# A two-weight spectral filter with a gate: a new order list with other read positions, a second unit with summed products, and four folds on GpSimd

## The chip, the cores and the metric

The kernel runs on one core of a Trainium2 chip. The metric is the device time of one execution in microseconds (us), the median of several runs. The core has a matrix engine (TensorE, PE in the profile), a vector engine (VectorE, DVE), an engine for activations and copies (ScalarE, ACT), a general one (GpSimd, POOL), and SyncE (SP), which here issues nearly all DMAs. Each engine takes its own instructions in program order and waits on semaphores for the others. Matrix products go to PSUM (eight banks of 128x512 f32); ScalarE and VectorE bring them back to SBUF, which is called evacuation here.

## The reference

Two spectral filters act on the same input, and a gate mixes them:

```python
def filt(x, w_r, w_i):                       # x: 1 x 2048 x 1024
    X = rfft2(x.astype(float32))
    X = X * (w_r + 1j * w_i)                 # weights: 2048 x 513
    return irfft2(X, s=(2048, 1024)).astype(bfloat16)

def reference(A_x, A_w_r, A_w_i, B_x, B_w_r, B_w_i, gate_w):
    x = A_x
    g = sigmoid((x * gate_w).sum(-1, keepdims=True))
    return g * filt(x, A_w_r, A_w_i) + (1 - g) * filt(x, B_w_r, B_w_i)
```

B_x is not used. All data are bf16.

## The kernel before

The transform of x is made once and multiplied by four weight planes (real and imaginary part of A and B). Column frequencies are split in an even half (par 0) and an odd half (par 1); row frequencies in 8 units for each half, so there are 16 units n, 0 to 7 even, 8 to 15 odd. The work has three stages.

- Head. x comes in 16 tiles. `V` (line 277, `xfold`) adds and subtracts the two column halves of a tile on VectorE; `f` is the first row transform of such a folded tile for both halves; `r` is the same from the raw tile, with matmuls of twice the width and no fold; `E` and `O` do one half each for a pair of tiles. The results are evacuated to y. `y` prepares the gate's weights.
- Units. `F` (f2, line 365) is the column transform of a unit, `G` (f3) the twiddle and second row transform, with the constant WF; `d` (edge) the products of an edge column; `c` (cmul, line 415) multiplies the unit by its four weight planes in one VectorE operation; `i n.r` (i1) is the first inverse row transform, real part r = 0 and imaginary r = 1, with the constant WI. `a` (part, line 439) adds two of the product planes on VectorE first, so that both i1 of that unit need three matmul terms instead of four. After `i n.1` the unit is written to a scratch in DRAM. For an even unit, GpSimd writes one column of the weights (L369) before `F`; it waits for the unit's weights. `h` and `g` make the gate and put it in the matrix EAB.
- Output. `q half.g.v` (fetch, line 470) reads the scratch back in another layout: q0 into xr (the memory of x), q1 into ro. `j half.v` (i2) is the second inverse row transform with the gate in it, `k` (i3) the inverse column transform, `s` (fold, line 551) adds and subtracts its cosine and sine parts, `D` (i3d) does k and s at once in matmuls for the odd half, `t` (last, lines 565 and 574) adds and subtracts the halves and writes to the output.

The order on every engine follows one list written out by hand, ORDER. Behind the colon stand the engines of a step's evacuations: A ScalarE, V VectorE; AV is first half and second half. In `k`, H leaves the sine part in PSUM for the fold to read there. For `s`, V is VectorE and Q is GpSimd, which cannot read PSUM. BANKS gives the PSUM bank of every product and SLOTS the buffer of every T, X, p, V and rl tile in order: there are two T, two X, four p, four V and four rl. A step that takes a buffer waits for its last readers.

SyncE issues in program order: x, then the constants and the weights W0 to W6 and W10 to W13 (lines 234 to 251), and then what the list says: the scratch writes, the late weights `w`, the reads `q`, the constant IGU (`l`), the outputs. A DMA whose condition isn't met holds back all behind it. Weights n = 7, 8, 9, 14, 15 reuse memory of x and of earlier weights. In the program, the reads q1.g.v need the scratch writes of four odd units: q1.0.v of units 8 to 11, q1.1.v of units 12 to 15; j1.0 and j1.1 need q1.0.0 and q1.1.0, j1.2 and j1.3 need q1.0.1 and q1.1.1, and so on.

Of the kernel before, what the change touches and what calls it, by code (L numbers as in the profile page):

```python
# [11 lines left out]
S = 2048  # L12
# [14 lines left out]


ORDER = """
V0 V1 V3 f0:AA f1:VA r2:AA V4 f3:VA V7 r5:AV V9 f4:AA r6:VA f7:VA r8:VA f9:VA r11:AA V13 r10:VA r12:AV f13:AA E14:VA y  # L30
O14:VA F0:AA F1:AA d0 G0:AA F2:AA d1 c0 G1:AA F3:AA d2 c1 G2:AA h F4:AA d3 G3:AA i0.0:AA i0.1:AA w7 c2 d4 c3 F5:AV
G4:AA i1.0:AA i2.0:VA c4 i2.1:AV d5 G5:AA i1.1:VA F6:AA F7:AA d6 w9 G6:AA i3.0:AA c5 i3.1:AV d7 F8:AA w8 c6 g0 i5.0:AA
G7:AV G8:AA w15 i5.1:AV q0.0.1 w14 c7 i6.0:AA q0.0.3 F9:AA F10:AA i4.0:AA c8 i6.1:VA i7.0:AA G9:AV G10:AV i4.1:VA
i7.1:AA c10 F11:AA q0.0.0 F12:AV c9 g1 G11:AA q0.0.2 c11 F13:AA G12:AA q0.1.0 i10.0:AA i9.0:AA i8.0:VA q0.1.3 i10.1:VV
i9.1:AA c12 i8.1:AA i11.0:VA G13:AA q0.1.1 q0.1.2 F14:VA F15:AA j0.0:AA c13 G14:AA i12.0:AV G15:AA i12.1:AA i11.1:AA
c14 c15 i13.0:AA i13.1:AA i14.0:AV a15.1:V i14.1:VV k0.0:HA j0.3:AA i15.0:AV i15.1:AV j0.2:AV j0.5:AA s0.0:V l q1.0.0
k0.3:HA j0.1:AA q1.1.0 s0.3:V j0.4:VA k0.5:HA j0.7:AA q1.0.1 s0.5:V k0.1:HA q1.1.1 k0.4:HA j0.6:AA s0.1:V k0.2:HA
s0.4:V q1.0.2 q1.1.2 k0.7:AA k0.6:HA j1.0:AA q1.1.3 s0.2:V j1.1:VA s0.6:V q1.0.3 k1.0:AA s0.7:V k1.1:HA s1.0:V j1.2:AA
j1.3:AA t0.2 s1.1:V D2:AA j1.4:AA k1.3:AA t2.2 t1.2 j1.5:AA s1.3:V D4:AA t3.2 t4.2 j1.6:AA D5:AA t5.2 D6:AA j1.7:AA
t6.0:S t6.1:S D7:AAAP t7.0:A t7.1:S  # L40
"""


# [1 line left out]


BANKS = """
01234567013245760321564371052634710562437162057143057623057146257146251427306517306514273065142763051427630154
62073154620731546207315426701354270615342706135427061354027364107236410752643071265401326470152647031564703125
64703125647  # L50
"""

SLOTS = {"T": "010101010101010101001010", "X": "0101010101001010", "p": "012302132103102130213021301",
         "V": "30123012302301230123", "rl": "0123012301231023102310321032103"}


def _bf16np(a):
# [99 lines left out]
def gated_mix(ctx, tc, x_in, we_in, wo_in, first_in, out):  # L157
    nc = tc.nc
    cn = make_constants()
    dr = {n: nc.inline_tensor(a, name=f"cst_{n.lower()}").ap() for n, a in cn.items() if n not in ("F1", "SG")}  # L160
# [13 lines left out]
    slots = {t: [wk.tile([P, w], BF16, name=f"{t}_{k}") for k in range(n)] for t, (n, w) in width.items()}  # L174
    order = {t: iter(v) for t, v in SLOTS.items()}

# [19 lines left out]
    F1 = const.tile([P, 208], BF16, name="f1")  # L196
# [10 lines left out]
    WF = const.tile([P, NT, 3, 64], BF16, name="wf")  # L207
    WI = const.tile([P, NT, 4, 64], BF16, name="wi")
# [5 lines left out]
    y = [Y[:, par] for par in range(2)]  # L214
# [3 lines left out]
    def load_w(n):  # L218
        par, u = n // NU, n % NU
        if n == 7:  # L220
            w = XP[0][:, 0:2064]
        elif 10 <= n < 14:
            w = wod[n - 10][:]
        else:
            k = {8: 0, 9: 1, 14: 2, 15: 3}.get(n, n)
            w = RP[k // 2][:, 2064 * (k % 2):2064 * (k % 2) + 2064]
        w = w[:, 0:8 * PIT[par]].rearrange("p (t a m) -> p t a m", t=2, a=4)
        nc.sync.dma_start(w, w_in[par][u])
        Ws[n] = w
# [4 lines left out]
    nc.sync.dma_start(fdv(0), dr["FD"][:, 0])  # L234
    nc.sync.dma_start(WF[:, 0:4], dr["WF"][:, 0:4])
    load_w(0)
    nc.sync.dma_start(WI[:, 0:4], dr["WI"][:, 0:4])
    load_w(1)
    load_w(2)
    nc.sync.dma_start(WF[:, 4:16], dr["WF"][:, 4:16])  # L240
    load_w(3)
    nc.sync.dma_start(WI[:, 4:16], dr["WI"][:, 4:16])
    load_w(4)
# [420 lines left out]
```

## Time and profile before

| | us |
|---|---|
| median of 3 runs (lowest, highest) | 107.3 (106.96, 108.08) |
| profiled execution | 107.58 |
| its span, first to last instruction | 105.8 |

| engine | busy us (share of the span) | instructions |
|---|---|---|
| TensorE | 96.9 (92%) | 1606 |
| VectorE | 90.7 (86%) | 141 |
| ScalarE | 93.6 (89%) | 187 |
| GpSimd | 10.1 (10%) | 14 |

The mean granted clock of TensorE is 0.996. The DMA queue of SyncE carried 36.37 MB in 16128 packets, 92.3% of the time of 16 DMA engines.

In the rows of the order of time, a row begins with its start and its length in us, merges neighbours of one kind (x16 is sixteen instructions), and ends with the idle time in front of it and what ended that idle time. An arrow reads output from input: `ro<-sc` is a read of the scratch into ro. Instructions of one engine overlap a little, so a ScalarE evacuation of 128x512 is 0.6 to 0.8 us long and the next starts 0.5 us after it. On ScalarE such rows are L263, on VectorE L265.

### The profile page before, as it was taken

What the parts mean: (1) busy time and instruction counts of PE and PEld (TensorE: products, weight loads), DVE (VectorE), ACT (ScalarE), POOL (GpSimd) and SP (SyncE); (2) the same over time, 40 slices, a digit from 0 to 9 for tenths busy, and PEclk for the clock granted to TensorE, in tenths of its full rate; (3) what the DMA queues carried; (4) which work ended last, traced back from release to release, by engine and by line L of the source; (5) the groups of instructions that cost most, each with busy time, mean ns of one, the idle gap of its engine ahead of it and who ended that gap; (6) DMA issues with size and microseconds to landing.
All of it is one profiled execution on the core that took longest, in us unless ns stands there. A gap on an engine that the chain in (4) does not pass through costs nothing. (4 is left out here: it accounts for less than half of the span.)

```text
span 105.8 us, 3917 instructions
## 1 busy us (share of the span) xinstructions
PE 96.9 (92%) x1606; PEld 66.5 (63%) x1608; DVE 90.7 (86%) x141; ACT 93.6 (89%) x187; POOL 10.1 (10%) x14
## 2 busy tenths in 40 slices
PE   5999999969999999999999999999999698999740
PEld 2299998635655766655765567667898485754520
DVE  1399877388999989999999999999989969899870
ACT  5069999997999999999999999999999888999730
POOL 1000001179880000000000000000000000000000
PEclk9999999999999999999999999999999999999998
DMA  2999999999999999999999799969999899967993
GB/s 50 395 421 421 386 358 353 413 428 396 398 405 409 401 375 359 395 356 345 386 373 403 223 376 379 373 249 340 321 278 298 338 353 418 397 259 321 389 352 120
DMA packets 16737, 37.06 MB, mean 350 GB/s; under 512 B 1612, under 2 KB 10448, under 8 KB 15696
## 3 DMA queue, kind: packets, MB, share of 16 engines
q1 hardware_dynamic: 16128, 36.37, 92.3%
q10 hardware_dynamic: 560, 0.45, 1.3%
q8 instruction: 12, 0.20, 0.7%
q14 instruction: 5, 0.04, 0.1%
q0 software_dynamic: 32, 0.00, 0.0%
HBM read 24.23 MB, written 12.58 MB: 348 GB/s over the span
## 5 line engine op out<-in xcount | busy, mean ns | idle before, releaser
L453 PE MATMUL pt<-p,wi 64*64 64x512 bf16 x504 | 30.1, 377 | 0.2 <-DVE rl L265 0.2
L263 ACT CAST rl<-pt 128x512 bf16<-128x512 f32 x47 | 25.9, 732 | 0.1
L415 DVE TENSOR_TENSOR p<-X,ro 128x4096 bf16<-128x4096 bf16 x11 | 25.2, 2297 | 0.4 <-ACT X L263 0.3
L263 ACT CAST T<-pt 128x512 bf16<-128x512 f32 (+1 forms) x40 | 21.8, 636 | 0.9 <-PE pt L532 0.5
L453 PEld LDWEIGHTS <-wi 64*64 64x64 bf16 x504 | 15.3, 106 | 10.4 <-issue 0.9
L263 ACT CAST V<-pt 128x512 bf16<-128x512 f32 x29 | 17.3, 748 | 1.1 <-PE pt L483 1.1
L263 ACT CAST X<-pt 128x512 bf16<-128x512 f32 x29 | 16.8, 682 | 0.1
L375 PE MATMUL pt<-fd,y 128*128 128x256 bf16 x128 | 15.9, 273 | 0.0
L263 ACT CAST y<-pt 128x512 bf16<-128x512 f32 x21 | 10.9, 649 | 3.9 <-PE pt L297 3.4
L375 PEld LDWEIGHTS <-y 128*128 128x128 bf16 x128 | 11.6, 98 | 4.2 <-issue 2.9
L265 DVE CAST rl<-pt 128x512 bf16<-128x512 f32 x17 | 11.3, 683 | 0.0
L498 PE MATMUL pt<-ig,V 128*128 128x256 bf16 x88 | 10.8, 273 | 0.0
L369 POOL TENSOR_SCALAR ro<-ro 128x8 bf16<-128x8 bf16 x7 | 8.7, 1244 | 21.4 <-DMA ro<-in_we_dram 21.4
L574 DVE TENSOR_TENSOR rl<-wo,T 128x1024 bf16<-128x1024 bf16 (+1 forms) x16 | 8.9, 620 | 0.6 <-ACT T L263 0.6
L394 PE MATMUL pt<-T,wf 64*64 64x512 bf16 (+2 forms) x192 | 9.4, 307 | 0.0
L263 ACT CAST p<-pt 128x512 bf16<-128x512 f32 x14 | 9.4, 823 | 0.0
L551 DVE TENSOR_TENSOR wo<-p,pt 128x512 bf16<-128x512 bf16 x14 | 8.8, 682 | 0.6 <-ACT p L263 0.5
L415 DVE TENSOR_TENSOR p<-X,wo 128x4096 bf16<-128x4096 bf16 x4 | 9.1, 2285 | 0.0
L498 PEld LDWEIGHTS <-V 128*128 128x128 bf16 x88 | 8.0, 98 | 1.5 <-issue 0.4
L265 DVE CAST y<-pt 128x512 bf16<-128x512 f32 x11 | 7.2, 686 | 0.4 <-PE pt L309 0.4
L306 PE MATMUL pt<-f,xr 64*128 64x256 bf16 x112 | 7.0, 269 | 0.0
L394 PEld LDWEIGHTS <-wf 64*64 64x64 bf16 x192 | 4.7, 107 | 3.0 <-issue 0.4
(58 smaller groups left out, 97.2 us busy)
## 6 DMA issues: line engine op xcount, KB each, us to landing
sc<-rl SPq DMA_DIRECT2D x16, 512.0 KB, 5.2
xr<-sc SPq DMA_DIRECT2D x8, 512.0 KB, 6.5
ro<-sc SPq DMA_DIRECT2D x8, 512.0 KB, 6.5
ro<-in_we_dram SPq DMA_DIRECT2D x7, 516.0 KB, 9.0
xr<-in_x_dram SPq DMA_DIRECT2D x7, 512.0 KB, 6.1
out_dram<-rl SPq DMA_DIRECT2D x6, 512.0 KB, 3.1
wo<-in_wo_dram SPq DMA_DIRECT2D x4, 512.0 KB, 7.5
ro<-in_wo_dram SPq DMA_DIRECT2D x4, 512.0 KB, 6.5
```

Of the source, the lines that this page charges most:

```text
L263: nc.scalar.copy(out=out, in_=in_)
L265: nc.vector.tensor_copy(out=out, in_=in_)
L306: nc.tensor.matmul(pv[h][:, :, c, :, :].rearrange("p a e k -> p e a k"), lhsT=xs(j0, h, q), rhs=fs(h, 0, *st), start=(q == 0), stop=(q == 3))
L369: nc.gpsimd.tensor_scalar(Ws[n][:, :, :, 257:258], Ws[n][:, :, :, 256:257], -1.0, None, ALU.mult)
L375: nc.tensor.matmul(ps[tt][:, e * 256:e * 256 + 256], lhsT=y[par][:, c, e, t].rearrange("p b s k -> p (b s k)"), rhs=FD[:, par, c, e, :], s ...
L394: nc.tensor.matmul(ps[tt][ho, dst:dst + ln], lhsT=WF[hp(j), 2 * u + tt, w, :], rhs=T[hp(j), tt, src:src + ln], start=(k == 0), stop=(k == 2))
L415: nc.vector.tensor_tensor(po, xo, wo, ALU.mult)
L453: nc.tensor.matmul(ps[tt][hp(j), :], lhsT=WI[hin, 2 * u + tt, w, :], rhs=p[hin, q, tt, a::2, o:o + 256], start=(k == 0), stop=(k == len(te ...
L498: nc.tensor.matmul(po, lhsT=V[:, s, 2 * r + c, :], rhs=IG[:, par, 2 * r + c, :], start=(c == 0), stop=(c == 1))
L551: (nc.vector if eng == "V" else nc.gpsimd).tensor_tensor(ev[:, :, r, :], c_, s_, op)
L574: nc.vector.tensor_tensor(o4[:, k, h] if not isinstance(od, list) else o4[:, k.start, h], x, y_, op)
```

## The change

The list ORDER is replaced as a whole, with its BANKS and SLOTS, and two constants change places in the SyncE queue. By count, the lists differ in this:

- `V` 7 to 6, `f` 7 to 6, `r` 7 to 8; the pair done by E and O is tiles 10 and 11 and not 14 and 15.
- `a` 1 to 2: units 1 and 5 in place of unit 15.
- `k` with H 8 to 2. `s` on VectorE 11 to 7; s0.0, s0.3, s0.5 and s0.7 are on GpSimd.
- `t1` goes out in halves.
- Evacuations on ScalarE 180 to 179, on VectorE 37 to 44, seven of these in `k`.
- All j and k stand behind i15.1 (before, j0.0, j0.3 and k0.0 stood ahead of it); the q1 reads stand in the list right behind it.
- WF[4:16] is issued ahead of W1, and WI[0:4] behind W2.

```diff
 ORDER = """
-V0 V1 V3 f0:AA f1:VA r2:AA V4 f3:VA V7 r5:AV V9 f4:AA r6:VA f7:VA r8:VA f9:VA r11:AA V13 r10:VA r12:AV f13:AA E14:VA y
-O14:VA F0:AA F1:AA d0 G0:AA F2:AA d1 c0 G1:AA F3:AA d2 c1 G2:AA h F4:AA d3 G3:AA i0.0:AA i0.1:AA w7 c2 d4 c3 F5:AV
-G4:AA i1.0:AA i2.0:VA c4 i2.1:AV d5 G5:AA i1.1:VA F6:AA F7:AA d6 w9 G6:AA i3.0:AA c5 i3.1:AV d7 F8:AA w8 c6 g0 i5.0:AA
-G7:AV G8:AA w15 i5.1:AV q0.0.1 w14 c7 i6.0:AA q0.0.3 F9:AA F10:AA i4.0:AA c8 i6.1:VA i7.0:AA G9:AV G10:AV i4.1:VA
-i7.1:AA c10 F11:AA q0.0.0 F12:AV c9 g1 G11:AA q0.0.2 c11 F13:AA G12:AA q0.1.0 i10.0:AA i9.0:AA i8.0:VA q0.1.3 i10.1:VV
-i9.1:AA c12 i8.1:AA i11.0:VA G13:AA q0.1.1 q0.1.2 F14:VA F15:AA j0.0:AA c13 G14:AA i12.0:AV G15:AA i12.1:AA i11.1:AA
-c14 c15 i13.0:AA i13.1:AA i14.0:AV a15.1:V i14.1:VV k0.0:HA j0.3:AA i15.0:AV i15.1:AV j0.2:AV j0.5:AA s0.0:V l q1.0.0
-k0.3:HA j0.1:AA q1.1.0 s0.3:V j0.4:VA k0.5:HA j0.7:AA q1.0.1 s0.5:V k0.1:HA q1.1.1 k0.4:HA j0.6:AA s0.1:V k0.2:HA
-s0.4:V q1.0.2 q1.1.2 k0.7:AA k0.6:HA j1.0:AA q1.1.3 s0.2:V j1.1:VA s0.6:V q1.0.3 k1.0:AA s0.7:V k1.1:HA s1.0:V j1.2:AA
-j1.3:AA t0.2 s1.1:V D2:AA j1.4:AA k1.3:AA t2.2 t1.2 j1.5:AA s1.3:V D4:AA t3.2 t4.2 j1.6:AA D5:AA t5.2 D6:AA j1.7:AA
-t6.0:S t6.1:S D7:AAAP t7.0:A t7.1:S
+V0 r1:AA f0:VV V5 V6 r3:AA r4:AV V8 f5:VA r2:VA f6:VA r7:AA f8:AA E10:VA r9:AA V13 V14 r12:VA f13:AA r15:VA f14:AV y
+O10:AA F0:VA F1:AA d0 G0:VA c0 F2:AA d1 G1:AA F3:AA d2 G2:AA F4:AA c1 i0.0:AA w8 d3 a1.0:V i0.1:AA d4 G4:AA c2 i1.0:AA
+c4 G3:AA w7 i1.1:AA F5:AA h F6:AA c3 d5 G5:VA c5 i2.0:AA i2.1:AA i3.0:VA i3.1:AV d6 a5.0:V G6:AA F7:AA w15 F8:AA c6
+i4.0:AV d7 w9 G7:AA i4.1:AA F9:VA q0.0.3 G8:AA i5.0:AA c7 i6.0:VA F10:AA q0.0.1 c8 G9:AA i7.0:AV G10:AA q0.0.2 i5.1:AV
+i7.1:AA c9 i6.1:VV c10 w14 F11:AA F12:AA g0 i8.0:AA i8.1:AA G12:VA i9.0:VA i9.1:VA q0.1.2 q0.1.1 G11:AA F13:AA F14:AA
+c12 q0.1.0 c11 i10.0:VA G13:AA q0.0.0 i12.0:AA c13 G14:AA F15:AA i11.0:AA q0.1.3 i11.1:AV i10.1:AV c14 G15:AA c15
+i13.0:AV i12.1:AA i13.1:AA g1 i14.0:AV i14.1:AA i15.0:AV i15.1:VA q1.0.0 j0.1:AV q1.0.1 q1.1.0 q1.1.1 q1.1.2 l j0.2:VA
+j0.0:VA j0.7:AV k0.1:VV j0.5:AA k0.2:HA j0.6:AA k0.0:VA s0.1:V s0.0:Q j0.3:VA k0.5:AA k0.6:HA s0.2:V j0.4:AA k0.3:AA
+q1.0.2 k0.7:AA s0.6:V s0.5:Q k0.4:VV j1.0:AA s0.4:V j1.1:AA q1.0.3 k1.0:VV q1.1.3 s1.0:V j1.2:AA k1.1:AA t0.2 j1.3:AA
+s1.1:V D2:AA t1.0:S j1.4:AA t1.1:S t2.2 k1.3:AA s1.3:V j1.5:AA D4:AA s0.3:Q j1.6:AA t3.2 D5:AA t4.2 t5.2 s0.7:Q D6:AA
+j1.7:AA t6.0:S t6.1:S D7:AAAP t7.0:A t7.1:S
 """
...
     nc.sync.dma_start(WF[:, 0:4], dr["WF"][:, 0:4])
     load_w(0)
-    nc.sync.dma_start(WI[:, 0:4], dr["WI"][:, 0:4])
+    nc.sync.dma_start(WF[:, 4:16], dr["WF"][:, 4:16])
     load_w(1)
     load_w(2)
-    nc.sync.dma_start(WF[:, 4:16], dr["WF"][:, 4:16])
+    nc.sync.dma_start(WI[:, 0:4], dr["WI"][:, 0:4])
     load_w(3)
     nc.sync.dma_start(WI[:, 4:16], dr["WI"][:, 4:16])
     load_w(4)
```

More of the change, by code (lines that the diff above doesn't have):

```diff
@@ L47 @@
 BANKS = """
-01234567013245760321564371052634710562437162057143057623057146257146251427306517306514273065142763051427630154
-62073154620731546207315426701354270615342706135427061354027364107236410752643071265401326470152647031564703125
-64703125647
-"""
-SLOTS = {"T": "010101010101010101001010", "X": "0101010101001010", "p": "012302132103102130213021301",
-         "V": "30123012302301230123", "rl": "0123012301231023102310321032103"}
+01234567012345617350264173502614735026147362735014736214507362145073162703162037614527615240376152403761524037
+56124750613247506134257061342706153427063125470612547036215473062517340516724051726403175264037152643071526430
+71526430715
+"""
+SLOTS = {"T": "010100101010110101010101", "X": "0101010101010101", "p": "012301230132010321032102323",
+         "V": "30123012301301230123", "rl": "012301230123012310232103210321"}
 def _bf16np(a):
```

## The prediction

> **What bounds it now.** I began with the page's busy shares: TensorE 92%, ScalarE 89%, VectorE 86%, the DMA engines at tenths of 9 nearly throughout. With three engines this full the question is where each of them still waits, so I read the order of time of each engine next. ScalarE first:
>
> ```profile
> 6.10 8.23 ACT L263 CAST y<-pt 128x512 bf16<-128x512 f32 x16 [3.44 <-PE pt L297]
> ...
> 25.27 0.58 ACT L344 CAST V<-pt 128x512 bf16<-128x512 f32 x1 [0.78 <-PE pt L341]
> ...
> 84.99 1.56 ACT L263 CAST V<-pt 128x512 bf16<-128x512 f32 x3 [0.66 <-PE pt L483]
> ...
> 88.48 2.05 ACT L263 CAST V<-pt 128x512 bf16<-128x512 f32 x4 [0.43 <-PE pt L483]
> ...
> 100.38 1.26 ACT L263 CAST T<-pt 128x256 bf16<-128x256 f32 x3 [0.26 <-ACT V L263]
> ```
>
> Columns: start, length, engine, line, operation, count, and in brackets the idle time before it. From 6.10 to 101.64 ScalarE idles about 3.0 us in all, of which these rows show 0.78, 0.66, 0.43 and 0.26. It is the chain that paces the kernel, and a wait that goes or comes on it is worth its length. TensorE gives the reasons:
>
> ```profile
> 14.80 1.95 PE L309 MATMUL pt<-f,xr 64*128 64x128 bf16 x64
> 16.73 1.91 PE L375 MATMUL pt<-fd,y 128*128 128x256 bf16 x16
> ...
> 22.71 0.20 PE L425 MATMUL pt<-T,wf 64*64 64x2 bf16 x4 [0.93 <-DMA wf<-cst_wf]
> ...
> 23.30 1.91 PE L341 MATMUL pt<-y,gwz 128*32 128x512 bf16 x32
> ...
> 74.53 1.11 PE L483 MATMUL pt<-eab,xr 128*128 128x64 bf16 x32
> ...
> 84.56 1.09 PE L483 MATMUL pt<-eab,ro 128*128 128x64 bf16 x32 [0.94 <-DMA ro<-sc]
> ...
> 88.05 1.09 PE L483 MATMUL pt<-eab,ro 128*128 128x64 bf16 x32 [0.45 <-DMA ro<-sc]
> ```
>
> The constant WF lands at 22.7, TensorE stands 0.93 us, the gate products (L341) come late, and that is ScalarE's 0.78. The reads of the odd half (ro<-sc) make TensorE stand 0.94 and 0.45, and that is ScalarE's 0.66 and 0.43. The profiled execution took 107.58 us, span 105.8; the median of the runs, 107.3, is 0.28 lower. I sum against 107.58 and take 0.28 off at the end.
>
> **Work that goes and comes.** Counted over both lists.
> - ScalarE: 180 plain evacuations become 179. Sixteen of them took 8.23 us, so they lie 0.5 us apart: -0.5, on the pacing chain.
> - TensorE: one raw `r` more and one folded `f` less. An `f` took 0.44 us (7.23 to 7.67), an `r` 0.88: +0.44. One more summed unit leaves out 8 of 32 matmuls, about 0.055 us each (112 in a row took 6.21): -0.44. Together 0.
> - VectorE: seven folds stay of eleven, two of them with a PSUM operand where eight had one. Six PSUM folds in a row took 3.68, 0.60 apart; two SBUF folds 0.75, 0.34 apart. Eleven cost 16 x 0.60 + 6 x 0.34 = 11.6, seven cost 4 x 0.60 + 10 x 0.34 = 5.8: -5.8. Seven more evacuations at 0.60: +4.2. One folding of x less, -0.7, one product sum more, +0.6, t1 in halves, +0.1. Together -1.6. VectorE is not the pacing engine, so this is cover and not gain.
>
> **Head of the list.** Now `r1` needs no folding and starts ScalarE 0.75 us earlier. But the last two x tiles were issued by 5.0 and took 9.6 us, so land at 14.6, and TensorE's 14.80 row already hugs that. In the new list V14 (x 14) stands on VectorE ahead of its evacuations of r12, r15 and f14, 0.6 each, so F0 comes at about 16.9 where it came at 16.73: 0, with +0.4 as the other end.
>
> **WF ahead of WI.** WF[4:16] passes W1, W2 and WI[0:4] on the SP queue, so lands about 4 us earlier (three transfers of 516, 516 and 256 KB at some 400 GB/s). WI[0:4] then lands about when WF did, 22.7, and i0.0 wants it at 23. W1 comes up to 1 us later, for d1, behind c0. So the 0.93 and with it ScalarE's 0.78 go: -0.8, other end 0. But what is late next? d4 now stands on VectorE before c2 (it stood after), and needs W4, which no reordering moves:
>
> ```profile
> 17.32 0.27 POOL L369 TENSOR_SCALAR ro<-ro 128x8 bf16<-128x8 bf16 x1 [16.29 <-DMA ro<-in_we_dram]
> ...
> 21.31 1.87 POOL L369 TENSOR_SCALAR ro<-ro 128x8 bf16<-128x8 bf16 x1 [1.00 <-DMA ro<-in_we_dram]
> 24.02 2.23 POOL L369 TENSOR_SCALAR ro<-ro 128x8 bf16<-128x8 bf16 x1 [0.83 <-DMA ro<-in_we_dram]
> ...
> 27.25 2.12 POOL L369 TENSOR_SCALAR ro<-ro 128x8 bf16<-128x8 bf16 x2 [0.32 <-DMA ro<-in_we_dram]
> ```
>
> One operation for each unit of the even half, released by its weights (W0, W2, W3, W4 and W5 here): W4 at 27.25. Then c2 starts at about 27.7 (26.73 before) and ends at 30.0; G3's evacuation needs the X slot c2 frees, and ScalarE gets there at about 29.2: +0.8. Ends: 0 if ScalarE is later, +1.3 if all of VectorE's wait passes on.
>
> **Reads that follow each other.** Two of the odd reads (q1.0.0, q1.0.1) now go out behind the last scratch write; only q1.1.0 waits for that write (issued 75.53, q1.1.0 at 80.32, data at 84.56). So j1.0's data still come some 10.0 us after TensorE's last i1 matmul. But j0.0, j0.3 and k0.0, which ran before that point, now lie behind it: eight j at 0.44 and eight k at 0.87 fill 10.5 us. j1.2's reads now stand one 512 KB transfer (1.3 us) nearer, at 12.2 instead of 13.5, where TensorE has 12.2 us of work. Both waits are covered: -1.1 on ScalarE, other end 0.
>
> **Four groups on GpSimd.** Eight sums of 128x512. The trace has no such row. Its memsets took 0.10 us for 1 element and 0.31 for 256, 0.82 ns an element: 0.52 us if three streams run side by side, 1.36 if in turn; I take 0.95, the middle, as nothing is nearer to either. GpSimd itself has room (10% busy, nothing after 40 us). The price lies on VectorE. Against the third and fourth rows above stand these:
>
> ```profile
> 20.75 2.30 DVE L415 TENSOR_TENSOR p<-X,ro 128x4096 bf16<-128x4096 bf16 x1
> ...
> 23.82 2.30 DVE L415 TENSOR_TENSOR p<-X,ro 128x4096 bf16<-128x4096 bf16 x1
> ```
>
> GpSimd's 0.27 us became 1.87 and 2.23, ending at 23.18 and 26.25, each 0.13 after the VectorE product ended: a VectorE operation with two SBUF inputs keeps GpSimd out until it is done. I take the same for the other direction, which no row shows. (The Trainium skill, "SBUF — State Buffer", section "Who interferes with whom", calls the pair of ports that the two share an exclusive lock that whichever starts first keeps for its whole instruction; the rows agree for VectorE first. Its "GPSIMD Engine Reference", section "Elementwise — side-by-side cycle accounting", has 2.6 cycles an element at 1.2 GHz, an estimate of 1.1 us for 512 elements; by that the sum below would be +0.1, not -0.35.) GpSimd is busy about 7.6 us from k0.0's evacuation on. In that time come VectorE's folds with both inputs in SBUF: s0.1, s0.4 and s1.0. At one blocked GpSimd operation for each: 3 x 0.95 = 2.85, less the 1.6 of cover: +1.25. Behind them on VectorE stand k1.0's evacuation and t0.2, and TensorE's banks behind those. Ends: 3 x 0.52 is inside the cover, 0; 4 x 1.36 - 1.6 = +3.8.
>
> **Sum.** -0.5 - 0.8 + 0.8 - 1.1 + 1.25 = -0.35: 107.2 in such an execution, 106.9 against the median.
>
> **Rivals.**
> - GpSimd's sums stay inside VectorE's cover. For it: VectorE idles 2.6 us in that stage as it is. -0.5 - 0.8 + 0.8 - 1.1 = -1.6: 105.7, down to 104.9 without the wait at G3. Chance 0.30.
> - Slower: GpSimd becomes VectorE's gate. Four waits of 1.36 make +3.8 in place of +1.25, so +2.2: 109.5. It decides from 3.2 us of blocked time on (1.6 of cover and 1.6 of gain), and is over 1% from 4.3. For it: a second fold of a pair finds the next GpSimd sum already queued; against: the folds from PSUM have one SBUF input. Chance 0.20.
> - The head loses: F0 0.4 later, W4's whole 1.3, ScalarE's 0.78 back by another wait. -0.5 + 0.4 + 1.3 - 1.1 + 1.25 = +1.35: 108.6. For it: VectorE now takes V6, V8 and V14 before evacuations that are ready. Chance 0.12.
> - The reads do pause: q1.1.0's wait is still there, and if j and k run faster than counted, -1.1 falls away: +0.75, 108.0. Chance 0.05.
>
> **How the numbers follow.** Forecast 106.9, chance 0.33, its own range 106.2 to 107.9. About 1% (1.1 us) is what a measurement here tells from no change. Faster by more: the first rival, 0.30. Within: forecast and last rival, 0.38. Slower: the other two, 0.32. The range 105.2 to 109.4 takes in the forecast, the head, the reads, most of the first rival and the near part of the second.
>
> **What would show it.** Right: no idle on ro<-sc before L483 near 84; no idle on WF near 22; ScalarE idle before an X evacuation near 29; GpSimd's L551 rows near 0.95 us, and L551 rows of VectorE from SBUF stretched beside them. Wrong: GpSimd's rows over 1.3 us with VectorE idle or stretched by more than 3.2 us after 78; F0 later than 17.2; or ScalarE's idle sum after 30 us above the 1.8 it has now, from banks or slots I did not follow.

## The result and the profile after

| | before | after |
|---|---|---|
| median, us (22 runs each, on the same chips) | 107.58 | 108.02 |
| ratio, 95% interval | | 1.0057 [1.0036, 1.0077] |
| profiled execution, us | 107.58 | 107.82 |
| its span, us | 105.8 | 105.7 |
| device time less span, us | 1.78 | 2.12 |

The change made the kernel slower by 0.6%, some 0.6 us. Four of the 22 runs of the kernel before (109.4 to 110.7 us) fell in a slower state and are left out of the ratio; the median of the others is 107.49. Half of the 0.6 us does not lie between the first and the last instruction at all: device time less span has a median of 2.11 us over the runs of the changed kernel (2.05 to 2.15), and of 1.77 to 1.79 over those of the kernel before. The span itself grew by 0.2 to 0.35 us in the medians (105.9 against 105.55 to 105.7 in the several series) and is about equal in the two profiled executions. So an equal span hides gains and losses that have to be found stage by stage.

The page of the changed kernel, first its engines with busy time and instruction counts, then the one new group of instructions:

```profile
PE 97.9 (93%) x1598; PEld 67.7 (64%) x1600; DVE 91.0 (86%) x141; ACT 93.2 (88%) x186; POOL 18.6 (18%) x22
...
L551 POOL TENSOR_TENSOR wo<-p 128x512 bf16<-128x512 bf16 x8 | 9.4, 1212 | 37.5 <-ACT p L263 37.5
```

GpSimd took eight sums off VectorE, and yet VectorE is as busy as before (91.0 against 90.7). Next the order of time of ScalarE after the change, the main rows with idle time from the head on:

```profile
11.42 7.21 ACT L263 CAST y<-pt 128x512 bf16<-128x512 f32 x14 [0.19 <-PE pt L306]
...
30.05 1.07 ACT L263 CAST X<-pt 128x512 bf16<-128x512 f32 x2 [0.38 <-DVE p L415]
...
76.21 1.07 ACT L263 CAST V<-pt 128x512 bf16<-128x512 f32 x2 [0.17 <-PE pt L483]
...
84.46 3.08 ACT L263 CAST V<-pt 128x512 bf16<-128x512 f32 x6 [0.32 <-PE pt L483]
...
90.79 1.07 ACT L263 CAST T<-pt 128x512 bf16<-128x512 f32 x2 [1.29 <-DVE rl L574]
```

The wait of 0.78 near 25 is gone, and those of 0.66 and 0.43 near 85 have shrunk to one of 0.32 (the 0.17 at 76.21 stands behind a product of the even half, which waits for no odd read). In their place stand 0.38 at 30.05 (the X evacuation of G3, which waits for c2) and 1.29 at 90.79. The second is the largest: the evacuation of D2 into a T buffer waits for VectorE's t0.2 (L574), which still reads it. With 0.62 us in three short waits of the head and 0.26 ahead of the last T the idle time adds up to 3.0 us, as before. TensorE in order of time:

```profile
14.89 0.44 PE L297 MATMUL pt<-f,rl 64*128 64x128 bf16 x9 [0.19 <-issue]
15.13 1.07 PE L306 MATMUL pt<-f,xr 64*128 64x256 bf16 x16
16.00 0.64 PE L297 MATMUL pt<-f,rl 64*128 64x128 bf16 x16
16.45 1.09 PE L309 MATMUL pt<-f,xr 64*128 64x128 bf16 x32
17.64 1.91 PE L375 MATMUL pt<-fd,y 128*128 128x256 bf16 x16
...
22.61 0.20 PE L425 MATMUL pt<-T,wf 64*64 64x2 bf16 x4
...
84.03 1.09 PE L483 MATMUL pt<-eab,ro 128*128 128x64 bf16 x32 [0.17 <-issue]
```

F0 (L375) begins at 17.64 where it began at 16.73: behind the last x tiles TensorE now has f13, r15, f14 and O10 in a row, from 14.9 on. At 22.61 nothing waits for WF. At 84.03 the first product of the odd reads waits 0.17 us where it waited 0.94. The row names nothing that ended this wait ("issue" means that the profile shows no releaser), but the time of the read does: q1.1.0, issued at 79.22, lands 4.7 us later, at 83.94, and the weight load of that product (PEld) starts 0.06 us after it:

```profile
84.00 1.00 PEld L483 LDWEIGHTS <-ro 128*128 128x128 bf16 x32 [0.42 <-issue]
```

In the kernel before, the same read lands at 84.42 and the load starts at 84.53. So the read still decides when the odd half begins; only the wait for it is shorter. And VectorE, in the stretch that leads up to ScalarE's 1.29:

```profile
83.46 1.29 DVE L265 CAST p<-pt 128x512 bf16<-128x512 f32 x2 [0.89 <-PE pt L498]
84.79 1.84 DVE L551 TENSOR_TENSOR wo<-p 128x512 bf16<-128x512 bf16 x2
...
87.86 1.51 DVE L551 TENSOR_TENSOR T<-p 128x512 bf16<-128x512 bf16 x2
89.41 1.29 DVE L574 TENSOR_TENSOR rl<-wo,T 128x1024 bf16<-128x1024 bf16 x2
```

A pair of folds from SBUF took 0.75 before. Here s0.4 takes 1.84 and s1.0 takes 1.51. GpSimd at that time, beside its earlier writes of weight columns:

```profile
27.02 0.43 POOL L369 TENSOR_SCALAR ro<-ro 128x8 bf16<-128x8 bf16 x1 [0.98 <-DMA ro<-in_we_dram]
...
79.32 9.43 POOL L551 TENSOR_TENSOR wo<-p 128x512 bf16<-128x512 bf16 x8 [37.53 <-ACT p L263]
```

Its eight sums run from 79.32 to 88.75 without a gap; the first stretched pair lies inside that time and the second begins in it. One by one, three of these four folds took 0.55, 1.37 and 1.17 us, and each ended 0.28 us after the end of a GpSimd sum; the fourth, behind the last sum, took 0.41, the usual time. Two of the sums beside them took 1.33 us in place of 1.15. The first row is W4, which lands near 27 as it did before.

### The profile page after: what moved, and what is told of

It is laid out like the page before. It is cut to its first block, busy times and chain, and to the rows that moved or that the text cites. A ratio compares the mean times of both kernels' runs of the same rounds, so it can differ in the third digit from the quotient of the medians.

```text
span 105.7 us, 3918 instructions
## 1 busy us (share of the span) xinstructions
PE 97.9 (93%) x1598; PEld 67.7 (64%) x1600; DVE 91.0 (86%) x141; ACT 93.2 (88%) x186; POOL 18.6 (18%) x22
## 4 chain that ended last, share of the span: by engine, by line
PE 87%; DVE 6%; ACT 2%; issue 1%; DVEq 0%; ACTq 0%
PE pt L453 27%; PE pt L375 14%; PE pt L498 9%; PE pt L394 7%; PE pt L483 7%; PE pt L532 7%; PE pt L306 5%; PE pt L195 3%; PE pt L297 2%; DVE y L265 2%; PE pt L341 2%; DVE rl L565 2%; PE pt L357 1%; ACT V L263 1%; DVE rl L574 1%
## 5 line engine op out<-in xcount | busy, mean ns | idle before, releaser
L263 ACT CAST rl<-pt 128x512 bf16<-128x512 f32 x47 | 28.4, 855 | 0.0
L263 ACT CAST T<-pt 128x512 bf16<-128x512 f32 (+1 forms) x41 | 23.0, 690 | 1.8 <-DVE rl L574 1.3
L263 ACT CAST X<-pt 128x512 bf16<-128x512 f32 x29 | 18.6, 774 | 0.4 <-DVE p L415 0.4
L375 PE MATMUL pt<-fd,y 128*128 128x256 bf16 x128 | 16.0, 273 | 0.1
L551 POOL TENSOR_TENSOR wo<-p 128x512 bf16<-128x512 bf16 x8 | 9.4, 1212 | 37.5 <-ACT p L263 37.5
L263 ACT CAST V<-pt 128x512 bf16<-128x512 f32 x27 | 15.0, 669 | 0.5 <-PE pt L483 0.5
L375 PEld LDWEIGHTS <-y 128*128 128x128 bf16 x128 | 11.5, 98 | 4.7 <-issue 3.3
L369 POOL TENSOR_SCALAR ro<-ro 128x8 bf16<-128x8 bf16 x7 | 7.0, 1000 | 22.4 <-DMA ro<-in_we_dram 22.3
L394 PE MATMUL pt<-T,wf 64*64 64x512 bf16 (+2 forms) x192 | 10.5, 307 | 0.1
L574 DVE TENSOR_TENSOR rl<-wo,T 128x1024 bf16<-128x1024 bf16 (+1 forms) x18 | 9.1, 568 | 0.6 <-ACT T L263 0.5
L306 PE MATMUL pt<-f,xr 64*128 64x256 bf16 x128 | 8.4, 279 | 0.0
L394 PEld LDWEIGHTS <-wf 64*64 64x64 bf16 x192 | 5.5, 106 | 3.9 <-issue 0.8
L306 PEld LDWEIGHTS <-xr 64*128 64x128 bf16 x128 | 6.2, 98 | 1.7 <-DMA xr<-in_x_dram 0.8
```

The source lines that it names most:

```text
L263: nc.scalar.copy(out=out, in_=in_)
L306: nc.tensor.matmul(pv[h][:, :, c, :, :].rearrange("p a e k -> p e a k"), lhsT=xs(j0, h, q), rhs=fs(h, 0, *st), start=(q == 0), stop=(q == 3))
L375: nc.tensor.matmul(ps[tt][:, e * 256:e * 256 + 256], lhsT=y[par][:, c, e, t].rearrange("p b s k -> p (b s k)"), rhs=FD[:, par, c, e, :], s ...
L394: nc.tensor.matmul(ps[tt][ho, dst:dst + ln], lhsT=WF[hp(j), 2 * u + tt, w, :], rhs=T[hp(j), tt, src:src + ln], start=(k == 0), stop=(k == 2))
L551: (nc.vector if eng == "V" else nc.gpsimd).tensor_tensor(ev[:, :, r, :], c_, s_, op)
L574: nc.vector.tensor_tensor(o4[:, k, h] if not isinstance(od, list) else o4[:, k.start, h], x, y_, op)
```

## The experiments

My theory after this reading: GpSimd's sums hold up VectorE's folds from SBUF, that passes on through the T buffer to ScalarE, and it eats what WF and the reads bring; the head's lateness is a second loss. Rivals: the wait is one for a buffer and goes with a third T; VectorE needs the relief, so that without GpSimd it would be worse; the head is the loss. Ratios are to the kernel before, with 95% intervals, spans are medians.

**The four groups back on VectorE.**

```diff
-s0.0:Q s0.5:Q s0.3:Q s0.7:Q
+s0.0:V s0.5:V s0.3:V s0.7:V
```

> The four folds go back from GpSimd to VectorE, in the changed list as it stands. If VectorE's folds s0.4 and s1.0 were stretched (1.84 and 1.51 us instead of 0.75) because GpSimd's sums held them, they take 0.75 again; but VectorE gets 4 x 0.67 = 2.7 us more, of which s0.3 and s0.7 stand late in the list: the last t is about 1 us later, ratio to the kernel before 1.010 to 1.020. If GpSimd had been no hindrance, the full 2.7 us show, 1.03. If the 0.3 us that the changed kernel has more outside its span (2.1 us against 1.8) come from GpSimd's eight sums, they are gone here.

Measured: 0.9935 [0.9905, 0.9965], 106.66 us, span 104.85, and 1.79 us outside the span. It is faster than both kernels, so my expectation was wrong, and so was the rival by which VectorE needs the relief. VectorE of this kernel:

```profile
85.11 0.76 DVE L551 TENSOR_TENSOR wo<-p 128x512 bf16<-128x512 bf16 x2
...
87.10 0.76 DVE L551 TENSOR_TENSOR T<-p 128x512 bf16<-128x512 bf16 x2
87.89 1.29 DVE L574 TENSOR_TENSOR rl<-wo,T 128x1024 bf16<-128x1024 bf16 x2
```

and its ScalarE:

```profile
89.28 1.07 ACT L263 CAST T<-pt 128x512 bf16<-128x512 f32 x2
```

Both pairs are back at 0.76, t0.2 begins 1.52 us earlier (87.89 against 89.41), and D2's evacuation follows at 89.28 with no wait, 1.51 earlier. VectorE does eight sums more here, about 2.7 us at the 0.34 apart of the prediction, and is busy 91.7 instead of 91.0: the 1.85 us by which GpSimd stretched its folds paid for most of that.

**The two stretched folds read PSUM.** With one input in PSUM a fold needs one evacuation less and takes 0.6 instead of 0.34.

```diff
-k0.4:VV k1.0:VV
+k0.4:HV k1.0:HV
```

> k0.4 and k1.0 leave their sine part in PSUM for the fold, so that s0.4 and s1.0 have one SBUF input. If GpSimd's sums hold only VectorE operations with two SBUF inputs, these folds take 2 x 0.60 us unstretched, t0.2 comes 1.5 to 2 us earlier, ScalarE's wait of 1.29 us for D2's buffer falls below 0.4, and the span shrinks by 0.5 to 1.2 us (ratio to before 0.995 to 1.001). If the wait for D2's buffer is a matter of the buffers or of VectorE's amount of work alone, nothing changes (1.006), for VectorE's work is the same within 0.1 us.

Measured: 0.9986 [0.9959, 1.0014], 107.21 us, span 104.9, 2.10 outside. VectorE and then GpSimd of this kernel:

```profile
84.87 1.28 DVE L551 TENSOR_TENSOR wo<-p,pt 128x512 bf16<-128x512 bf16 x2
...
87.75 1.29 DVE L551 TENSOR_TENSOR T<-p,pt 128x512 bf16<-128x512 bf16 x2
```

```profile
79.69 9.07 POOL L551 TENSOR_TENSOR wo<-p 128x512 bf16<-128x512 bf16 x8 [37.94 <-ACT p L263]
```

GpSimd's eight sums still run beside both pairs (to 88.76, 0.3 us before the second pair ends), and the pairs take 1.28 and 1.29, what PSUM pairs took before the change (1.28). D2's wait is gone, and the span is that of the kernel without GpSimd, 104.9 against 104.85. So it is not GpSimd as such that costs span here, but GpSimd beside folds that take both inputs from SBUF.

**A third T buffer, which D2 takes.**

```diff
-"T": (2, 1024)
+"T": (3, 1024)
-"T": "010100101010110101010101"
+"T": "010100101010110101210101"
```

> D2 gets a third T buffer, so that its evacuation need not wait until t0.2 has read the old one. The stretch of s0.4 and s1.0 stays at about 1.9 us. If the buffer is the whole way by which the stretch reaches the end, ScalarE's 1.29 us wait goes and the span shrinks by about 1 us; if VectorE itself is full by then (it idles only 0.47 and 0.19 us after 84.8), the wait goes and the span shrinks by 0.2 to 0.6 us at most.

Measured: 1.0006 [0.9979, 1.0032], 107.37 us, span 105.5, 1.91 outside. The folds are stretched as before (1.85 and 1.51), D2 does not wait, but ScalarE does a little later:

```profile
96.17 2.30 ACT L263 CAST T<-pt 128x512 bf16<-128x512 f32 x4 [0.87 <-DVE rl L574]
```

The buffer is how the delay gets from VectorE to ScalarE, not where it comes from: with it taken away two thirds of the wait (0.87 of 1.29) come back at the next T.

**Two of the four groups on GpSimd** (s0.0 and s0.5 stay, which come first).

```diff
-s0.3:Q s0.7:Q
+s0.3:V s0.7:V
```

> The changed kernel with s0.0 and s0.5 on GpSimd and s0.3 and s0.7 on VectorE again. GpSimd is then done at about 83.9 us, before VectorE's folds with two SBUF inputs come (84.8 and later). If only the meeting costs, s0.4 and s1.0 take 0.75 us again and the span is that of the kernel without GpSimd (104.5) or up to 0.7 us less; time outside the span shows what the presence of GpSimd's sums costs: 0.1 to 0.35 us. If GpSimd's sums cost something wherever they stand, the ratio stays near 1.000.

Measured: 0.9996 [0.996, 1.0031], 107.27 us, span 105.2, 2.08 outside. GpSimd is done at 84.55 us, the pairs behind it take 0.76 each, and D2 does not wait: no meeting, no stretch, as expected. The span, expected at 104.5 or below, lies 0.35 us above that of the kernel without GpSimd and 0.7 below that of the changed kernel; the 0.35 is no larger than span differences that stay unexplained further down, so it is not put down to the two groups.

**One group on GpSimd in the kernel before.**

```diff
-s0.7:V
+s0.7:Q
```

> The kernel before with one group, s0.7, on GpSimd, two sums of 128x512. If full-sized late sums lengthen the time outside the span, 1.9 to 2.1 us; s1.0, the next VectorE fold, has one SBUF input here and should not be stretched, so the span stays within 0.3 us of before.

Measured: 0.9965 [0.9931, 0.9999], 107.25 us, span 105.4 (median), 1.79 outside. GpSimd:

```profile
83.83 2.26 POOL L551 TENSOR_TENSOR wo<-p 128x512 bf16<-128x512 bf16 x2 [43.88 <-ACT p L263]
```

One group costs nothing and may bring 0.3%. VectorE of this kernel folds from PSUM until 84.5 and then waits 1.10 us for TensorE. So where no fold from SBUF runs beside them, these sums on GpSimd show no price.

**The head of the kernel before.** Its first lines replace the new ones, first with the banks of before, then with banks renamed so that the steps behind it find the same ones free as in the changed kernel.

```diff
-V0 r1:AA f0:VV V5 V6 r3:AA r4:AV V8 f5:VA r2:VA f6:VA r7:AA f8:AA E10:VA r9:AA V13 V14 r12:VA f13:AA r15:VA f14:AV y
-O10:AA
+V0 V1 V3 f0:AA f1:VA r2:AA V4 f3:VA V7 r5:AV V9 f4:AA r6:VA f7:VA r8:VA f9:VA r11:AA V13 r10:VA r12:AV f13:AA E14:VA y
+O14:VA
```

> The head of the list (x foldings, f, r, E, O, with their banks and buffers) is that of the kernel before, the rest as changed. If the head costs what its rows show (F0 at 17.64 us instead of 16.73), F0 is back at 16.7 to 16.8 and the end comes 0.6 to 0.9 us earlier: ratio to before 0.998 to 1.000. If the head is hidden behind a later wait (the reads or D2's buffer), the end moves less than 0.2 us.

> The changed kernel with the head of the kernel before, its eight banks renamed so that F0 and F1 find the same banks free as in the changed list (the earlier try left F1 waiting 0.72 us for a bank). If the 0.9 us by which F0 is late reach the end, F0 is at 16.7 to 16.9, no wait at F1, and the ratio to the kernel before falls from 1.006 to 0.997 to 1.000. If ScalarE's 1.3 us wait for D2's buffer, set by VectorE and GpSimd, or the weights' arrival take it back, 1.003 to 1.006.

Measured: 1.0033 [1.0008, 1.0057] and 1.0022 [0.9996, 1.0049], spans 105.6 and 105.7. In the first, F1 waits 0.72 us for a bank, so only the second is read. There TensorE has F0 at 16.70, 0.94 earlier:

```profile
16.70 1.91 PE L375 MATMUL pt<-fd,y 128*128 128x256 bf16 x16
```

And ScalarE at G3:

```profile
30.05 1.07 ACT L263 CAST X<-pt 128x512 bf16<-128x512 f32 x2 [1.16 <-DVE p L415]
```

with VectorE at d4, ahead of c2:

```profile
27.48 0.28 DVE L430 TENSOR_TENSOR p<-pt,ro 128x8 bf16<-128x8 f32 x2 [0.81 <-POOL ro L369]
```

The evacuation of G3 starts at 30.05 in both kernels. It waits 1.16 us here and 0.38 there, and from it on the times are the same (i15.1 at 69.03, the first odd product at 84.03, the last matmul at 100.98). So the head's 0.9 us is real and brings nothing in these two executions: W4 lands near 27, d4 waits for its column on VectorE (it starts at 27.48 here and at 27.49 in the changed kernel), c2 stands behind d4, and G3 needs the X buffer that c2 frees. The other traces agree: in seven profiled executions with d4 ahead of c2 and F0 between 16.70 and 17.93, G3's evacuation starts at 30.00 to 30.15. There is an end to it. In three others F0 came at 18.68 to 18.89, and there G3's evacuation starts without a wait at 30.55 to 30.72. Part of that lateness lies in TensorE's first two steps: r1 and f0 took 2.3 and 2.5 us in the two of these with the changed head, where the changed kernel took 1.8. A head that late does cost.

**The old head without GpSimd** (both edits).

> The changed list with the old head (banks renamed) and the four folds on VectorE. Without GpSimd the changed list was at 0.9935 of the kernel before. If the head is worth its 0.9 us, 0.985 to 0.988; if VectorE, which is full from 78 us on there, decides the end whatever the head does, the shift still passes through, since VectorE's start shifts as well; 0.9935 would mean that something with a fixed time, such as the weights' or the reads' arrival, decides.

Measured: 0.9947 [0.9913, 0.9981], 106.88 us, span 105.1. No better than without GpSimd alone (0.9935), so the runs show no gain from the old head there either. The profiled execution is one of the three with a late F0 (18.89), so its trace cannot show why.

**c2 ahead of d4**, so that c2 does not wait for W4; in the kernel without GpSimd, with the new head and with the old.

```diff
-i0.1:AA d4 G4:AA c2 i1.0:AA
+i0.1:AA c2 d4 G4:AA i1.0:AA
```

> Without GpSimd's folds (0.9935 of the kernel before), c2 moved ahead of d4 on VectorE, so that it no longer waits for W4. With the changed head VectorE comes to c2 at about 27.3 us anyway where it now starts at 27.6, so 0.3 us at most: ratio 0.990 to 0.994, and ScalarE's 0.46 us wait at 30 us mostly gone.

> As the run beside it, and with the old head too (banks renamed), which on its own left the instant 30.05 us of G3's evacuation as it was. If W4, by way of d4, c2 and the X buffer, is what swallowed the head's 0.9 us, G3's evacuation now comes at about 29.2 us without a wait and the end 0.7 to 1.0 us earlier than in the run beside it: ratio 0.983 to 0.988. If something else pins the list, the same as beside it.

Measured: 1.0119 [1.0071, 1.0167], span 107.05, and 1.0071 [1.003, 1.0113], span 106.3: both slower, a miss. TensorE of the first:

```profile
30.45 0.69 PE L394 MATMUL pt<-T,wf 64*64 64x512 bf16 x12 [1.47 <-DVE p L430]
```

Now G3's own matmuls wait for d4 (L430), since G3 takes the banks out of which d4 reads. But d4 does not wait for W4 any more. GpSimd and VectorE of the same kernel:

```profile
27.03 0.27 POOL L369 TENSOR_SCALAR ro<-ro 128x8 bf16<-128x8 bf16 x1 [2.60 <-DMA ro<-in_we_dram]
```

```profile
28.00 2.30 DVE L415 TENSOR_TENSOR p<-X,ro 128x4096 bf16<-128x4096 bf16 x1
30.20 0.26 DVE L430 TENSOR_TENSOR p<-pt,ro 128x8 bf16<-128x8 f32 x2
```

W4's column is written at 27.30, and d4 starts at 30.20, when c2 with its 2.30 us is done. In the kernel with the old head c2 runs from 26.49 to 28.78, holds GpSimd's write of the column until 28.90, and d4 starts at 28.94. The exchange took the wait for W4 away and put c2 in front of G3's banks, which is longer.

**The same with the banks of G3 and i1.1 exchanged**, with the old head and without GpSimd.

> No GpSimd folds, old head, c2 ahead of d4, and G3 takes the bank pair of i1.1, since in the run with c2 first TensorE waited 1.47 us at G3 for d4, which still read G3's banks. If bank and buffer together were what pinned the list to W4's arrival, that wait is gone and the ratio is 0.984 to 0.990; if the next wait on W5 or on d4 pins it as well, 0.993 to 0.996.

Measured: 1.0032 [0.9997, 1.0067], span 105.7: a miss. The wait for d4 goes to i1.1, which got those banks:

```profile
29.34 0.93 PE L453 MATMUL pt<-p,wi 64*64 64x512 bf16 x12 [1.28 <-DVE p L430]
```

Here too d4 starts (at 29.09) when c2 is done, over 2 us after W4 has landed. So these three tries show what c2 ahead of d4 costs, and none of them shows what the list would gain if W4 came earlier. Whether another list could keep the head's time was not found out.

**The order of the constants alone**: the old one in the changed kernel, and the new one in the kernel before.

```diff
-WF[4:16] ahead of W1, WI[0:4] behind W2
+WI[0:4] ahead of W1, WF[4:16] behind W2
```

> The changed kernel with WI[0:4] issued ahead of WF[4:16] as before. WF then lands at 22.7 us, and the step that needs it (d2) now stands at 22.61, since the whole list is 0.9 us late there: the change of order should be worth at most 0.1 us (ratio 1.005 to 1.007). By the sum of the prediction, which gave it 0.8 us, the ratio would be 1.013.

> The kernel before with WF[4:16] ahead of W1 and WI[0:4] behind W2, nothing else. TensorE's 0.93 us wait for WF at 22 us goes, and with it ScalarE's 0.78: by the prediction's term 0.8 us of gain (ratio 0.993). If the later W1 and W2 hold d1 and d2 on VectorE instead, or a later wait (the odd reads at 84 us) takes it back, 0.998 to 1.001.

Measured: 1.0072 [1.0043, 1.0101], 108.08 us, which the noise does not tell from the changed kernel (1.0057), and 0.9981 [0.9956, 1.0007], 107.29 us. In the kernel before, the wait for WF goes as forecast, and i0.0 starts at 25.64 instead of 26.61. But ScalarE then has a wait of 0.27 at 26.22 and a longer one behind it,

```profile
42.85 1.07 ACT L263 CAST X<-pt 128x512 bf16<-128x512 f32 x2 [0.66 <-DVE p L415]
```

and VectorE, ahead of that,

```profile
40.27 0.27 DVE L430 TENSOR_TENSOR p<-pt,xr 128x8 bf16<-128x8 f32 x2 [1.44 <-POOL xr L369]
```

that is, a wait for W7 (0.48 us in the kernel before). The first product of the odd reads then starts at 84.86, behind its read, where it was at 84.56. Of 0.97 us at i0.0 about 0.2 us arrive at the end in the median, and the interval of the ratio reaches to no gain at all.

**What sets the time outside the span.** First, whether GpSimd's work as such does it: eight sums of 128x8 on GpSimd in the kernel before, once at the start, once in the output stage.

```diff
+for k in range(8):
+    nc.gpsimd.tensor_tensor(gj[:], gj[:], gj[:], ALU.add)
```

> The kernel before, and in its first microsecond eight GpSimd sums of 128x8 on a tile of their own, which nobody waits for. The span should not move. If the presence of such sums makes the time outside the span longer (1.78 us before, 2.11 in the changed kernel), it is 1.9 to 2.1 here and the ratio 1.001 to 1.003; if it is where or how late they stand, 1.78 and 1.000.

> The kernel before with eight GpSimd sums of 128x8 behind k0.7 (near 85 us), into a tile that nobody reads. Eight such sums in the first microsecond left the time outside the span at 1.78 us. If late GpSimd sums make it longer whatever their size, it is 1.9 to 2.1 here, the span within 0.1 us of before, ratio 1.001 to 1.003. If it is their size or their writing to data that is used, 1.78.

Measured: 0.9994 [0.9962, 1.0027] with 1.78 outside, and 1.0023 [0.9989, 1.0058] with 1.77 outside. It does not. Nor does one whole group (1.79, above), while the kernel of the exchanged banks, which has no such sum, has 1.95. Set against the number of instructions that each compiled program holds for ScalarE, waits and branches included (the page's ACT x186 counts those that work alone), the kernels fall into groups:

| instructions for ScalarE | kernels so far | outside the span, us |
|---|---|---|
| 308 | before, its constants exchanged, its three with GpSimd sums | 1.77 to 1.79 |
| 310, 311 | without GpSimd, with the old head too, c2 first | 1.75 to 1.80 |
| 312 | old head (both), banks exchanged | 1.94 to 1.97 |
| 313 | changed kernel, PSUM folds, two groups, old constants | 2.08 to 2.11 |
| 314 | third T buffer | 1.91 |

So the last three runs change that number and no other work, with one-element activations at the start, where ScalarE waits for x: five more in the kernel before (313), one more in the changed kernel (314), four more there (317).

```diff
+for _ in range(5):
+    nc.scalar.activation(junk[:], warm[:, 0:1], ACT.Sigmoid)
```

> The kernel before with five more one-element ScalarE activations at its start, where ScalarE waits for x anyway (2.66 to 6.10): 313 instructions on ScalarE where it had 308. If the count of ScalarE's instructions sets the time outside the span, that time goes from 1.78 to about 2.1 us at an unchanged span (105.6), ratio 1.003. If the GpSimd sums or anything else of the changed list set it, it stays at 1.78.

> The changed kernel with one more such activation: 314 instructions on ScalarE where it had 313. By the count, the time outside the span falls from 2.11 to about 1.91, as with the third T buffer, which had 314 too: 107.8 in place of 108.0. By any other reading it stays at 2.11.

> The changed kernel with four more such activations: 317 on ScalarE. No kernel had this count, so the theory of the count gives only that the time outside the span may differ from 2.11; if the bump at 312 to 314 is a narrow one, it is back at 1.78 and the kernel at 107.7. By any other reading it stays at 2.11.

ScalarE of the first:

```profile
2.46 1.38 ACT L259 ACTIVATE junk<-V 128x1 f32<-128x1 bf16 x6
5.86 6.62 ACT L264 CAST y<-pt 128x512 bf16<-128x512 f32 x13 [2.02 <-PE pt L298]
```

The added work ends 2 us before ScalarE's first evacuation. Measured outside the span: 2.13 us (2.08 to 2.17), 1.94 (1.88 to 1.97) and 1.98 (1.76 to 2.11), where the kernel before on the same chip has 1.77 (1.73 to 1.85). The first two are what the count forecast, and the first makes the kernel before as slow outside its span as the changed one. The third is not back at 1.78, and it spreads more than any other. Whole times: 1.0059 [1.0018, 1.0099], 1.0092 [1.0059, 1.0126] and 1.0044 [1.0007, 1.0082]. The second expectation, 107.8 us, missed: 108.3, since the span was 106.35 there, 0.45 above the changed kernel's. Also the first has 0.35 us more span in the median, but not in its profiled execution (105.6). These span differences are not explained; the profiled execution of the second is one of the three with a late F0 (18.70). They set a scale: span differences below about 0.45 us between two kernels here are not put down to a cause.

## Why the prediction failed in sign

The forecast was 106.9 us, faster by 0.4 us; measured was 108.02, slower by 0.6%. That lies inside the range, but the sign is wrong. The kernel without GpSimd divides the difference in three, by medians of the span: from about 105.6 before to 104.85 without GpSimd is -0.75, where the terms of the prediction without GpSimd make -1.6; the four groups add 1.05 to that (105.9), where it had +1.25; and 0.33 lies outside the span, where it had nothing. So two steps failed. The time outside the span was put at nothing, and the runs with idle activations show what that missed. And the gains of the list were put at 1.6 where the medians have 0.75. Of this second error two parts are seen: the reads brought less (0.8 us of waits went and not 1.1, since q1.1.0 still sets the start of the odd half), and WF's 0.8 brings nothing measurable in the changed list (the run with the old constants). The rest stays open.

**GpSimd, +1.25: the mechanism right, the sum close by luck, the working half wrong.** The wait that it makes on ScalarE is 1.29, and taking the four groups out is worth 1.05 of span. The row that the prediction did not have, VectorE held up by GpSimd, is now there, and the run with PSUM folds shows what decides it. (The Trainium skill, "SBUF — State Buffer", section "Who interferes with whom", has the lock in both directions; the trace agrees, with 0.75 to 1.84 us for a pair. By the Trainium skill, "GPSIMD Engine Reference", section "Elementwise — side-by-side cycle accounting", the estimate for a sum was 1.1 us; the rows have 1.15 to 1.33, so that was nearer than the 0.95 that was taken.) But two groups of folds were held up and not three, for 1.09 + 0.76 = 1.85 us and not 2.85: s0.1 at 78.84 was ahead of GpSimd's start. And the 1.6 us of cover did not cover: VectorE's idle time of 0.89 lies ahead of the stretched folds (at 83.46), where nothing is late yet, and between them and D2's buffer there is none. Two errors of about the same size cancelled.

**WF ahead of WI, -0.8, with W4's +0.8 behind it: the waits were there, but they do not add up.** WF's wait and ScalarE's 0.78 are gone. Yet with the constants in the old order the changed kernel takes 108.08 us, no measurable amount more: the step that needs WF stands at 22.61 now, within 0.1 us of where WF landed before. The constants alone in the kernel before brought about 0.2 us of 0.97. c2 ends so that G3's evacuation starts at 30.05, where the prediction had 30.0; ScalarE's wait there is 0.38, and 1.16 with the head in time, where the prediction had 0.8. It had ScalarE there at 29.2, and with the old head that is 28.9 (30.05 less 1.16). Of the 1.16, VectorE's wait for W4's column is 0.81. Here a wait on the pacing chain was worth its length only up to the next arrival that the queue sets.

**Head, 0: wrong by 0.9 us, and without effect at that size.** F0 came at 17.64, past the 17.2 that was named as a sign of a wrong step. What was missed is the work of TensorE that stands behind the last x tiles (f13, r15, f14, O10). In the profiled execution it had no price, as the wait at G3 became shorter by as much (0.78); the run with the old head and renamed banks shows that.

**Reads, -1.1: too large, and the cover was not complete.** 1.09 us of waits became 0.32, so -0.8 by these rows. The read q1.1.0 landed 11.0 us after TensorE was done with i1 (83.94 against 72.97) and not 10.0; the read itself took 4.7 us where it took 4.1 before. TensorE had 10.9 us of work to put ahead of it, so the odd half still begins when that read lands.

**ScalarE's evacuation, -0.5, and VectorE's -1.6 as cover** were not tried by themselves. ScalarE's waits of the two profiled executions can be set against each other: WF -0.78, reads -0.77, G3 +0.38, D2 +1.29, the rest -0.08, together +0.04. With one evacuation less that would be a gain of about 0.5 us; ScalarE's last evacuation ends 0.24 earlier (101.40 against 101.64), and the spans are 105.7 and 105.8. The medians of the span differ by 0.2 to 0.35 the other way. For the kernel without GpSimd, too, the profiled executions are 1.3 apart and the medians 0.75. So these rows do not account for the sign of the span difference, and that stays open; it is no larger than the span differences without an explanation above.

**Not in the sum: 0.33 us outside the span.** I summed against 107.58 with 1.78 outside as if that were fixed. The changed program has 313 instructions for ScalarE in place of 308: one evacuation less, six waits more. That five instructions more on ScalarE can make this difference is shown by the kernel before with five idle activations (2.13). Two of those six waits go with the GpSimd sums (without them there are 311, and 1.79 outside). This is nearly as much as the whole gain that was forecast (0.35).

Of the rivals, the one in which GpSimd's sums stay inside the cover (105.7) is refuted by the stretched folds and by the run without GpSimd. The one in which GpSimd gates VectorE was sized for 3.2 us of blocked time, of which 1.85 came. The one in which the head loses had the right two parts, F0 late and W4's whole wait, but added them, and they are the same time. The one in which the reads do pause, with the chance of 0.05, was right that q1.1.0's wait is still there, though only 0.32 of it reaches ScalarE. ScalarE's idle time after 30 us rose to 2.4 from the 1.8 that was named as a limit.

## What to carry to other kernels

Before work is handed to GpSimd to relieve VectorE, list the VectorE instructions that will run in the same time and take both inputs from SBUF: each can be held until the running GpSimd operation ends (a fold of 0.42 us took up to 1.37 here), while those that read PSUM lost nothing here; idle time of VectorE can cover it only where it lies between the blocked instruction and its reader. Where one instruction is moved ahead of another to escape a wait, look at what the other then waits for: c2 ahead of d4 put 2.3 us where a wait of 0.8 had been. Where a late transfer sets a step's time (W4 here), gains and losses ahead of it are not to be added up, as only the largest lateness counts. And where a change is worth a few tenths of a per cent, look at device time less span too, and at the number of instructions of each engine, waits included.

## What the runs showed that was not expected

The time outside the span depends on the program: 1.75 to 1.80 us with 308, 310 and 311 instructions for ScalarE, 1.94 to 1.97 with 312, 2.08 to 2.13 with 313 and 1.91 to 1.94 with 314 in the medians; with 317 the median is 1.98 and single runs lie between 1.76 and 2.11. Five activations at the start of the kernel before made as much as the changed list's six waits more and one evacuation less, which lie elsewhere. Why the number matters, and whether that of another engine does too, stays open.

A bf16 sum of 128x512 took GpSimd 1.15 us (1.15 to 1.33) where a fold in SBUF takes VectorE 0.42; beside it a single VectorE fold took up to 1.37.
